# Transposing attention outputs by DMA instead of TensorE, with a new order for the first two batches

## The chip, the cores and the metric

One core of a Trainium2 chip. The metric is the device time of one execution in microseconds (us). "Span" is the time from first to last instruction in a profiled execution; the time measured from outside is some 2 us longer. A TensorE clock that the throttle lowers is shown in the profile as "PEclk".

## The reference, cut to what matters

```python
# q, k, v: [8 batches, 8 heads, 576 positions, 64]; 16 beacon keys and values for each head
scores = q @ concat(beacon_k, k).T / 8          # causal for k, the beacons are always visible
x = softmax(scores) @ concat(beacon_v, v)       # -> [4608 tokens, 512]
h = x @ w_in                                    # 512 -> 2048
out = maximum(0.01 * h, h) @ w_out              # 2048 -> 512
```

## The kernel before: the parts that matter

The kernel handles two heads at a time; such a group is called g0 to g31, four to a batch. Attention gives `x_nat`, with tokens in the partitions. The first feed-forward product needs `xT`, with channels in the partitions, so each group is transposed once: five TensorE transposes into PSUM (the memory that TensorE writes its results to), one VectorE copy out.

```python
def x_transposes(g):
    b, hp = divmod(g, NPAIR)
    x_nat, _ = xs.pop(g)
    ps = ps_one.tile([128, 1024], BF16, name="tp", tag="one")
    for t, (q0, rows) in enumerate(QT):      # QT: (0,112) (112,128) (240,128) (368,128) (448,128)
        nc.tensor.transpose(ps[:, q0:q0+rows], x_nat[0:rows, t]..., ident[0:rows, 0:rows])
    nc.vector.tensor_copy(out=xT[:, hp, b*S:(b+1)*S], in_=ps[:, 0:S])
```

The feed-forward part is cut into "fills", each four matmuls of 512 columns, which the schedule places between attention steps so that TensorE always has work. A fill of the first product reads `xT` of all four groups of a batch, so it may only be placed after that batch is released (`ready`).

```python
def fill():
    ...
    can1 = i1 < ready[0] and (i1 < 2 or i2 > i1 - 2)    # first product of chunk i1 (512 tokens)
    can2 = i2 < NCH and i2 < i1                         # second product of an earlier chunk
    ...
def finish(g):
    x_transposes(g)
    if hp == NPAIR - 1:
        ready[0] = NCH if b == B - 1 else b + 1
# for g: score(g); finish(g-3); value(g-2); t_q(g+1); masks(g), and fills in eight slots from g6 on
```

The kernel fixes the order of each engine's instructions by hand. SyncE's queue carries the loads of v and the stores of results (36 of 128x512 float32). GpSimd's queue carries the loads of q, k and the weights.

The softmax here doesn't subtract the row's maximum and nothing guards it: scores larger than these inputs give would overflow.

## Time and profile before

| | before |
|---|---|
| median time of 4 executions | 378.03 us (377.18 to 380.02) |
| span of the profiled execution | 375.6 us, mean granted clock 0.995 |
| TensorE wait for `xT` (copied by VectorE) | 2.1 us in all |
| filled group, eight fills | 9.81 us |
| unfilled group | 3.86 us |

A filled group is a group of attention with eight fills in it, an unfilled one has none. The prediction below shows the lines behind most of this table and reads them.

### The profile page before, as it was taken

To read this page: it belongs to the slowest core of one execution; us is meant where nothing else is said; L and a number is where in the kernel's file an instruction comes from. 1 tells how busy PE (TensorE), PEld (TensorE's weight loads), DVE (VectorE), ACT (ScalarE), POOL (GpSimd) and SP (SyncE) were. 2 spreads that over 40 slices of the span, in tenths; PEclk is the share of its full clock that TensorE was granted. 3 is DMA by queue.
4 is the path that set the end of the run, shared out by engine and by line. 5 is a ranking of instruction groups with operands and counts; after the bars stand their busy time and mean duration, and the time that the engine had idled before them with its cause. 6 is when DMAs were issued, how large, how long until landed. Compare 5 with 4: busy or idle time off the path is not lost.

```text
span 375.6 us, 7715 instructions
## 1 busy us (share of the span) xinstructions
PE 356.3 (95%) x3264; PEld 187.5 (50%) x3264; DVE 172.8 (46%) x402; ACT 195.4 (52%) x308; POOL 103.5 (28%) x143
## 2 busy tenths in 40 slices
PE   4887899999998899999999999999999999999996
PEld 4565464444555455555554555555554554444442
DVE  2779742243558645555456536644554332000021
ACT  3948574376436684368634763487336701643300
POOL 8569226684204802171208202300000000000000
PEclk9999899999999999999999999999999999999999
DMA  8997999959119910178015901100010011001012
GB/s 173 171 223 119 197 203 191 210 107 152 60 61 226 168 18 30 54 125 163 3 58 115 198 2 57 58 2 2 28 58 30 1 45 70 0 0 58 28 56 84
DMA packets 58370, 33.82 MB, mean 90 GB/s; under 512 B 41440, under 2 KB 53472, under 8 KB 58336
## 3 DMA queue, kind: packets, MB, share of 16 engines
q0 software_dynamic: 13152, 13.34, 22.8%
q1 hardware_dynamic: 44896, 19.67, 21.3%
q8 instruction: 25, 0.41, 0.5%
q10 hardware_dynamic: 288, 0.33, 0.3%
q14 instruction: 9, 0.07, 0.1%
HBM read 37.22 MB, written 9.44 MB: 124 GB/s over the span
## 4 chain that ended last, share of the span: by engine, by line
PE 86%; DVE 7%; DMA 3%; POOL 2%; SPq 1%; issue 1%; ACT 0%
PE acc L385 34%; PE acc L369 33%; PE av L333 7%; PE sc L267 6%; PE tp L244 4%; PE tp L355 2%; DMA v_raw<-in_k_dram 1%; DMA v_raw<-in_v_dram 1%; DVE osb L394 1%; DVE xT L360 1%; POOL q_raw L137 1%; DVE x_nat L343 1%; DVE qT L249 1%; SPq L216 1%; DVE kT L249 1%; DVE aT L299 1%
## 5 line engine op out<-in xcount | busy, mean ns | idle before, releaser
L369 PE MATMUL acc<-xT,w_in_sb 128*128 128x512 bf16 x576 | 140.6, 380 | 2.1 <-DVE xT L360 2.1
L278 ACT ACTIVATE aT<-sc 128x928 bf16<-128x928 f32 (+2 forms) x128 | 102.3, 855 | 75.9 <-PE sc L267 75.8
L385 PE MATMUL acc<-w_out_sb,gT 128*128 128x512 bf16 x576 | 139.1, 379 | 0.0
L376 ACT ACTIVATE gT<-acc 128x512 bf16<-128x512 f32 x144 | 85.7, 600 | 81.9 <-PE acc L369 81.8
L369 PEld LDWEIGHTS <-w_in_sb 128*128 128x128 bf16 x576 | 52.4, 98 | 59.8 <-issue 3.8
L385 PEld LDWEIGHTS <-gT 128*128 128x128 bf16 x576 | 52.1, 98 | 60.0 <-issue 5.3
L394 DVE COPY osb<-acc 128x512 f32<-128x512 f32 x36 | 24.8, 690 | 93.5 <-PE acc L385 93.1
L267 PE MATMUL sc<-qT,kT 64*128 64x128 bf16 (+5 forms) x384 | 42.6, 309 | 6.9 <-DVE kT L249 3.3
L333 PEld LDWEIGHTS <-aT 128*128 128x128 bf16 (+1 forms) x960 | 38.9, 100 | 16.5 <-issue 3.2
L333 PE MATMUL av<-v_aug,aT 128*128 128x65 bf16 (+1 forms) x960 | 42.0, 197 | 1.1 <-DVE xT L360 0.8
L167 POOL COPY q_nat<-q_raw 128x1152 bf16<-128x1152 bf16 (+1 forms) x16 | 18.3, 1145 | 82.5 <-PE tp L244 52.2
L249 DVE COPY qT<-tp 128x576 bf16<-128x576 bf16 x32 | 24.2, 755 | 33.7 <-PE tp L244 33.7
L343 DVE TENSOR_TENSOR x_nat<-av,rec 128x384 bf16<-128x384 f32 x64 | 31.4, 491 | 2.2
L267 PEld LDWEIGHTS <-kT 64*128 64x128 bf16 (+1 forms) x384 | 18.1, 100 | 21.1 <-issue 11.9
L225 POOL CAST v_aug<-v_raw 128x512 bf16<-128x512 f32 (+1 forms) x30 | 19.4, 683 | 33.5 <-PE av L333 31.5
L360 DVE COPY xT<-tp 128x576 bf16<-128x576 bf16 x32 | 14.5, 452 | 29.4 <-PE tp L355 29.4
L342 DVE RECIPROCAL rec<-av 128x6 f32<-128x6 f32 x64 | 11.8, 185 | 33.1 <-PE av L333 33.1
L137 POOL DMA_DIRECT2D q_raw<-in_q_dram x31 | 20.7, 669 | 12.3 <-DMA v_raw<-in_v_dram 4.5
L249 DVE COPY kT<-tp 128x576 bf16<-128x576 bf16 x31 | 23.2, 748 | 0.0
L299 DVE TENSOR_TENSOR aT<-aT,mask 128x768 bf16<-128x768 bf16 x32 | 22.6, 705 | 1.3 <-ACT aT L278 1.3
L137 POOL DMA_DIRECT2D k_raw<-in_k_dram x31 | 19.6, 632 | 7.4 <-DMA w_out_sb<-in_moe_w_out_dram 5.6
L167 POOL COPY k_nat<-k_raw 128x1152 bf16<-128x1152 bf16 (+1 forms) x16 | 18.5, 1157 | 0.9 <-DMA k_raw<-in_k_dram 0.9
(33 smaller groups left out, 149.7 us busy)
## 6 DMA issues: line engine op xcount, KB each, us to landing
out_dram<-osb SPq DMA_DIRECT2D x36, 256.0 KB, 2.0
v_raw<-in_v_dram SPq DMA_DIRECT2D x24, 256.0 KB, 6.2
q_raw<-in_q_dram POOLq DMA_DIRECT2D x31, 144.0 KB, 6.0
k_raw<-in_k_dram POOLq DMA_DIRECT2D x31, 144.0 KB, 6.2
w_in_sb<-in_moe_w_in_dram POOLq DMA_DIRECT2D x4, 512.0 KB, 8.6
w_out_sb<-in_moe_w_out_dram POOLq DMA_DIRECT2D x4, 512.0 KB, 16.8
v_raw<-in_v_dram SPq DMA_DIRECT2D x8, 224.0 KB, 4.6
v_raw<-in_v_dram SPq DMA_DIRECT2D x8, 160.0 KB, 5.1
```

The costliest lines, as they stand in the source:

```text
L137: dma = nc.gpsimd.dma_start(out=dst[e * RP : (e + 1) * RP], in_=src[b, h0 : h0 + 2].rearrange("h (p i) d -> p h i d", i=RI),)
L167: copy(out=dst[p0:p1], in_=src[p0:p1].rearrange("p h i d -> p i h d"))
L249: copy(out=dst.rearrange("c (p i) -> c p i", i=RI), in_=ps[:, 0:S].rearrange("c (i p) -> c p i", i=RI),)
L267: nc.tensor.matmul(out=sc[0 : ROWS[c], par, col - c0 : col - c0 + w], lhsT=kT[ps_, c * 128 : c * 128 + ROWS[c]], rhs=qT[ps_, q0 : q0 + w], ...
L278: last = nc.scalar.activation(out=aT[:, :, c0 : c0 + w], in_=sc[:, :, 0:w], func=AF.Exp, scale=0.125)
L299: nc.vector.tensor_tensor(out=diag, in0=diag, in1=tri[:, None, None, :].to_broadcast([128, 2, 3, 128]), op=ALU.mult,)
L333: nc.tensor.matmul(out=avv[:, n, 0 : D + 1], lhsT=aT[0 : ROWS[c], par, a0 : a0 + 128], rhs=va[0 : ROWS[c], c, 2 * hp + par, :], start=(c = ...
L343: nc.vector.tensor_tensor(out=x_nat[:, t0:t1].rearrange("p t e d -> p (t e) d"), in0=avv[:, :, 0:D], in1=rec[:, n0:n1, None].to_broadcast( ...
L369: nc.tensor.matmul(out=acc, lhsT=w_in_sb[:, j, fc * 128 : (fc + 1) * 128], rhs=xT[:, j, i * 512 : (i + 1) * 512], start=(j == 0), stop=(j ...
L376: nc.scalar.activation(out=gT[i][:, fc, :], in_=acc, func=AF.Prelu, alpha=0.01)
L385: nc.tensor.matmul(out=acc, lhsT=gT[i][:, fc, t * 128 : (t + 1) * 128], rhs=w_out_sb[:, fc, :], start=(fc == 0), stop=(fc == NF - 1),)
L394: nc.vector.tensor_copy(out=osb, in_=acc)
```

## The change

The intent is to take 160 transposes off TensorE and 32 copies off VectorE by letting DMAs that transpose while they copy (called the crossbar here) write `xT` straight from `x_nat`. To leave the DMAs time, a batch is released one group later, and the first eight groups and the v load of batch 2 are put in a new order.

```diff
-        ps = ps_one.tile(...)
-        for t, (q0, rows) in enumerate(QT):
-            nc.tensor.transpose(...)
-        nc.vector.tensor_copy(out=xT[:, hp, b * S : (b + 1) * S], in_=ps[:, 0:S])
+        flat = x_nat.rearrange("p t e d -> p t (e d)")
+        dst = xT[:, hp, b * S : (b + 1) * S]
+        nc.sync.dma_start_transpose(out=dst[:, None, 0:112], in_=flat[0:112, 0])
+        nc.sync.dma_start_transpose(
+            out=dst[:, 112:496].rearrange("p (t q) -> p t q", t=3),
+            in_=flat[:, 1:4].rearrange("p t x -> p (t x)"),
+        )
+        nc.sync.dma_start_transpose(out=dst[:, None, 448:576], in_=flat[:, 4])
...
-                ready[0] = NCH if b == B - 1 else b + 1
+                nxt[0] = NCH if b == B - 1 else b + 1     # ready[0] = nxt[0] at the next group
...
+            if g < 2 * NPAIR:        # new order of the first eight groups
+                score(g, 0); score(g, 1); t_q(g+1); value(g-2, 0); score(g, 2); score(g, 3)
+                value(g-2, 1); finish(g-3); masks(g)     # fills only from g7 on, in effect
```

(The last lines are condensed. Also: a third `x_nat` buffer; half of the first kT copies on ScalarE; `load_v(2)` after `finish(7)` instead of in g3; the casts of v for batches 1 and 2 and the transposes of the beacon keys also move by a group or so.)

More of the change, by code (lines that the diff above doesn't have):

```diff
@@ L319, in value @@
             xs[g] = (
-                headpool.tile([128, 5, 2, D], BF16, name="x_nat"),
+                headpool.tile([128, 5, 2, D], BF16, name="x_nat", bufs=3),
                 headpool.tile([128, 10], FP32, name="rec"),
@@ L352, in x_transposes @@
         x_nat, _ = xs.pop(g)
-        ps = ps_one.tile([128, 1024], BF16, name="tp", tag="one")
-        for t, (q0, rows) in enumerate(QT):
-            nc.tensor.transpose(
-                ps[:, q0 : q0 + rows],
-                x_nat[0:rows, t].rearrange("p e d -> p (e d)"),
-                ident[0:rows, 0:rows],
-            )
-        nc.vector.tensor_copy(out=xT[:, hp, b * S : (b + 1) * S], in_=ps[:, 0:S])
+        flat = x_nat.rearrange("p t e d -> p t (e d)")
[6 more added lines that the diff above has]
+        nc.sync.dma_start_transpose(out=dst[:, None, 448:576], in_=flat[:, 4])
     gT = {}
@@ L471, in loads @@
                 for i in range(4):
-                    w = load_w_out(i)
-                load_v(2, after=w)
+                    load_w_out(i)
                 load_qk(2, 0)
@@ L484, in loads @@
                         permute(b + 1, hp - 2, which, nc.gpsimd.tensor_copy)
-                if hp == 3:
+                if hp == 3 and b > 1:
                     cast_v(b + 1, nc.gpsimd)
@@ L492, in finish @@
             if hp == NPAIR - 1:
-                ready[0] = NCH if b == B - 1 else b + 1
-        for g in range(NG + 3):
+                nxt[0] = NCH if b == B - 1 else b + 1
+        nxt = [0]
+        for g in range(NG + 4):
+            ready[0] = nxt[0]
             if has(g):
@@ L517 @@
                 finish(g - 1)
+                load_v(2)
+                ready[0] = nxt[0]
                 for n in range(16):
@@ L535 @@
                 masks(g)
+                cast_v(2, nc.gpsimd)
                 fill()
+                continue
+            if g < 2 * NPAIR:
+                score(g, 0)
+                score(g, 1)
+                if g == 3:
+                    beacon_transposes(1, B)
+                if g + 1 < 2 * NPAIR:
+                    t_q(g + 1, 0)
+                    t_q(g + 1, 1, nc.scalar.copy if g % 2 else nc.vector.tensor_copy)
+                slot(2)
+                if g != 2 and has(g - 2):
+                    value(g - 2, 0)
+                slot(3)
+                score(g, 2)
+                score(g, 3)
+                if g == 2:
+                    cast_v(0, nc.vector)
+                    value(0, 0)
+                slot(5)
+                if has(g - 2):
+                    value(g - 2, 1)
+                slot(6)
+                if g == NPAIR:
+                    cast_v(1, nc.vector)
+                if has(g - 3):
+                    finish(g - 3)
+                masks(g)
                 continue
@@ L543 @@
             slot(0)
-            if g == 2:
-                cast_v(0, nc.vector)
-            if g == NPAIR + 1:
-                cast_v(1, nc.vector)
             if has(g - 3) and not 2 * NPAIR < g <= 2 * NPAIR + 2:
@@ L564 @@
             slot(5)
-            if g == 2:
-                beacon_transposes(1, B)
             slot(6)
```

## The prediction

> **What bounds the kernel now.** I read the page's busy shares and its chain of waits first.
>
> ```profile
> PE 356.3 (95%) x3264; PEld 187.5 (50%) x3264; DVE 172.8 (46%) x402; ACT 195.4 (52%) x308; POOL 103.5 (28%) x143
> ...
> PE 86%; DVE 7%; DMA 3%; POOL 2%; SPq 1%; issue 1%; ACT 0%
> PE acc L385 34%; PE acc L369 33%; PE av L333 7%; PE sc L267 6%; PE tp L244 4%; PE tp L355 2%; DMA v_raw<-in_k_dram 1%; DMA v_raw<-in_v_dram 1%; DVE osb L394 1%; DVE xT L360 1%; POOL q_raw L137 1%; DVE x_nat L343 1%; DVE qT L249 1%; SPq L216
> ```
>
> TensorE carries 86% of the chain, two thirds of the span with the feed-forward product alone. The transposes that the change removes (tp L355) are 2% of it. "Busy" counts each matmul's latency, so I took real cost from starts in the timeline of TensorE (start, us, what), in a group of heads in the steady part:
>
> ```profile
> 131.61 1.04 PE L369 MATMUL acc<-xT,w_in_sb 128*128 128x512 bf16 x4
> 132.48 0.44 PE L355 MATMUL tp<-ident,x_nat 112*128 112x112 bf16 x5
> 132.76 1.03 PE L369 MATMUL acc<-xT,w_in_sb 128*128 128x512 bf16 x4
> ```
>
> Five transposes hold the queue for 132.76 - 132.48 = 0.28 us. A "fill" (four 512-column matmuls) holds it 0.865 us (330.33 to 331.19, and so on in the tail). Then the windows view, one row for each group g of two heads, cut at its first score matmul (window, length, busy us of TensorE, weight loads, VectorE, ScalarE, GpSimd, granted clock, DMA share, GB/s):
>
> ```profile
> 23.69:29.84 6.15, 5.01 (x68) 3.78 (x67) 5.94 (x12) 3.47 (x5) 3.67 (x4) 1.00 0.91 164
> 29.84:33.70 3.86, 3.14 (x67) 2.22 (x67) 3.79 (x12) 3.38 (x5) 3.86 (x6) 1.00 0.52 73
> 33.70:39.23 5.53, 3.19 (x65) 2.35 (x67) 5.46 (x17) 3.39 (x5) 5.26 (x6) 0.95 1.24 205
> 39.23:46.88 7.65, 7.65 (x81) 4.19 (x82) 5.37 (x16) 5.26 (x8) 1.18 (x2) 0.81 1.23 195
> 46.88:52.62 5.74, 5.74 (x65) 3.09 (x65) 2.61 (x8) 5.42 (x9) 1.23 (x3) 1.00 1.23 203
> ...
> 117.11:120.97 3.86, 3.15 (x65) 2.37 (x67) 3.79 (x12) 3.49 (x6) 0.94 (x3) 1.00 1.25 253
> 120.97:131.09 10.12, 9.11 (x93) 4.74 (x94) 7.20 (x16) 6.94 (x11) 8.69 (x15) 1.00 1.07 172
> 131.09:140.90 9.81, 9.81 (x99) 5.13 (x99) 4.16 (x11) 7.81 (x13) 0.97 (x1) 1.00 0.15 25
> ```
>
> There are two regimes. A group with eight fills lasts 9.81 us and TensorE never idles. A group without fills (29.84, 117.11) lasts 3.86 us, VectorE busy for 3.79 of it: VectorE is the limit there, ScalarE next at 3.4 to 3.5, while TensorE's own attention work is about 9.81 - 8 x 0.865 = 2.9 us. So the removed matmuls count in the filled groups, the removed VectorE copies in the others.
>
> **What the Trainium skill says.** "VectorE: DVE Perf Modes", The three transpose paths, gives 390 ns for a TensorE transpose of 128x128 and 1309 ns for the DMA crossbar. The trace has 218 ns median latency per transpose and only 0.28 / 5 = 0.056 us of queue time, so the saving is far smaller than the page's duration suggests. For the crossbar this trace has nothing. "DMA: Bandwidth & Descriptors", Latency and other measured facts, gives 261 GB/s for one transposing kernel: 147 KB for a group is then an estimated 0.6 us plus a fixed part, against 9.8 us between groups. The same page, Issuing engines are not separate DMA queues, says all queues interleave on the same 16 engines. The trace agrees: 256 KB to the output lands in 2.0 us median when the engines are idle, a 256 KB piece of v takes 6.2 us. "TensorE: Matmul & The Clock Gate", Part 1, says the array runs at half rate until it has been busy some 3.4 us. The trace fits: nine q transposes start over 0.48 us at 25.91 (to 26.38) and 0.27 us at 31.10 (to 31.37), though the granted clock reads 1.00 in both windows.
>
> **The change part by part.** *Removed:* 160 transposes, 32 x 0.28 = 9.0 us of TensorE queue, nearly all in the path; and 32 VectorE copies of 0.452 us, 14.5 us in all, hidden except in unfilled groups, where one takes 0.37 us of the sequence (31.09 to 31.46). *Added:* 96 transposing DMAs on SyncE's queue, three per group. The third overlaps the second's destination (448 to 495) and by the build's order waits for it, so a group's SyncE chain is about one landing plus issue; I guess 3 to 4 us under load. *Moved:* batch 2's v load goes behind the last of batch 1's transposes; half of the first groups' kT copies go to ScalarE (0.64 us); scores go ahead of values; and a batch's transposed outputs are released one group later.
>
> That delay moves fills. Walking the counters of the schedule: before, no fills in g0 to g5, four each in g6 and g7, four in g12, none in g13, seven in g14. After: none in g0 to g6, four in g7, eight in g12, none in g13 and g14. Both have given 64 fills when g13 starts; after has still given 64 when g15 starts, which is where before stands at g14.
>
> I build the end time from the windows:
> 1. To g4. It cannot start much before 29.84: batch 1's first k block is only permuted by GpSimd at 24.78 + 1.15 = 25.93, behind its load, and that load is not moved. I take 29.3.
> 2. g4 to g6, no fills, VectorE the limit: 3 x (3.86 - 0.37) + 1.68 (v cast) - 0.67 (one kT copy to ScalarE) = 11.5; with 0.5 for a cold array g7 starts at 41.3. Before it was 46.88 with four more fills done, worth 3.5.
> 3. g7: 5.74 - 0.28 = 5.46, so g8 at 46.8 (before 52.62).
> 4. g8 to g12: before 117.11 - 52.62 = 64.5; less five transposings (1.4), less an idle 0.74 of the half-starved g12, plus the four late fills (3.46): 65.8. g13 at 112.6.
> 5. g13, g14 unfilled: 2 x 3.5 = 7.0. g15 at 119.6.
> 6. The rest: before, 375.6 - 120.97 = 254.6 from g14 with the same fills to go. Less one group's attention, 9.81 - 6.92 - 0.28 = 2.6; less 21 transposings, 5.9; less 1.2 of TensorE waits for the VectorE copy of xT (1.01 in g14 and 0.22 at 317): 244.9. End at 364.5.
>
> I add 1.5 for waits on transposing DMAs at g7 and in g8: 366.0 of span. Time exceeded span by 377.99 - 375.6 = 2.4, so 368.4, rounded to 368: 2.6% faster.
>
> **The rivals.** *(a) The transposes land late in the head.* The DMA share reads 0.9 to 1.2 there, and the first fill in g7 (about 42) needs groups 0 to 3. Their chain starts behind batch 1's v (issued until 22.9); my guess lands group 3 at about 43. If a chain takes 6 to 7 us instead, group 3 lands near 52 and group 7 near 77 (needed near 60 plus the first delay): 10 to 15 us lost, time 378 to 385. For it: congestion, and a chain of dependent DMAs. Against it: the crossbar moves half the bytes of one 256 KB load, and three x_nat buffers decouple it. *(b) Longer starvation lets the array go cold*, as at 39.23, where four fills and a group took 7.65 us at clock 0.81. Seven unfilled groups at the start and two in a row later could cost 2 to 4 us: 370 to 372. *(c) The gain is hidden:* if VectorE or DMA arrivals set the filled stretch, nothing is saved. The 9.81 us row with TensorE at 9.81 and VectorE at 4.16 speaks against it. *(d) The head gains more:* scores ahead of values and the later beacon transposes could remove the hole at 21.3 to 22.8; 364. Step 1's load speaks against it.
>
> **Range and chances.** The 9 us are well founded; the head is worth about +2 minus DMA waits. Rivals (b) and (d) give 364 to 372, (a) a tail above. Range 362 to 377; 2% faster means below 370.4. Chances: faster 0.64, same 0.27, slower 0.09.
>
> **What would show it.** In the page after: no L355 matmuls and no xT copy; a filled group at 9.5 us; g7, g13 and g15 near 41, 113 and 120; unfilled groups near 3.5. A TensorE wait for the transposes of xT over 3 us in g7 or g8 makes (a) right; two groups near 4.5 at g13 and g14, or matmuls at half rate there, make (b) right. A filled group still at 9.8 would make the prediction wrong at its root.

## The result

The changed kernel takes 407.38 us (406.5 to 409.89, four executions) against 378.03 us. The ratio is 1.0779 (95% interval 1.0713 to 1.0844): 7.8% slower. A ratio is always the mean time of one kernel's fast runs over that of the other's in the same rounds, so it is not quite the ratio of the medians quoted here.

First the page of the changed kernel: busy shares, the time line of TensorE and its clock in 40 slices of 10.2 us, the chain that ended last, and the costliest matmul group.

```profile
PE 351.7 (86%) x3059; PEld 180.4 (44%) x3104; DVE 158.5 (39%) x367; ACT 197.0 (48%) x311; POOL 101.5 (25%) x143
...
PE   5776305949999991999999999999999999999996
...
PEclk9999555997999995799999999999999999999999
...
PE 71%; DMA 13%; DVE 6%; SPq 5%; ACT 2%; issue 2%; DVEq 0%; ACTq 0%
...
L369 PE MATMUL acc<-xT,w_in_sb 128*128 128x512 bf16 x555 | 142.2, 390 | 35.5 <-DMA xT<-x_nat 33.9
```

The last of these lines in the kernel before:

```profile
L369 PE MATMUL acc<-xT,w_in_sb 128*128 128x512 bf16 x576 | 140.6, 380 | 2.1 <-DVE xT L360 2.1
```

TensorE's share of the chain fell from 86% to 71%, and DMA with SyncE's queue now hold 18%. The last line of the changed page says where: the first product's matmuls stood idle 35.5 us, 33.9 of them waiting for transposing DMAs. Before, they waited 2.1 us for VectorE's copy. In slices 5 to 7 and 16 the granted clock is 0.5 and TensorE is at most half busy.

The timeline of TensorE (start, us, what, idle before) shows the first fill in g7. Its four matmuls read groups 0, 1, 2 and 3 in turn:

```profile
43.31 0.61 PE L369 MATMUL acc<-xT,w_in_sb 128*128 128x512 bf16 x1
49.09 0.58 PE L369 MATMUL acc<-xT,w_in_sb 128*128 128x512 bf16 x1 [5.18 <-DMA xT<-x_nat]
59.06 0.58 PE L369 MATMUL acc<-xT,w_in_sb 128*128 128x512 bf16 x1 [9.39 <-DMA xT<-x_nat]
66.03 0.59 PE L369 MATMUL acc<-xT,w_in_sb 128*128 128x512 bf16 x1 [6.39 <-DMA xT<-x_nat]
```

Each waits for one group's transposes: 5.18 + 9.39 + 6.39 = 21.0 us in one fill. The queue of SyncE in the same time shows why. L355, L356 and L360 are a group's three transposing DMAs; a row's length is the time of issue:

```profile
33.16 1.27 SPq L355 DMA_TRANSPOSE xT<-x_nat  x1
34.52 1.27 SPq L356 DMA_TRANSPOSE xT<-x_nat  x1
43.65 1.11 SPq L360 DMA_TRANSPOSE xT<-x_nat  x1
44.84 1.18 SPq L355 DMA_TRANSPOSE xT<-x_nat  x1
46.12 1.21 SPq L356 DMA_TRANSPOSE xT<-x_nat  x1
53.63 1.11 SPq L360 DMA_TRANSPOSE xT<-x_nat  x1
54.79 1.23 SPq L355 DMA_TRANSPOSE xT<-x_nat  x1
```

The third transpose overwrites columns 448 to 495 of the second, so it is issued only after the second has landed, that is, after its data have arrived: 34.52 + 1.27 = 35.79 to 43.65 is 7.9 us, then 47.33 to 53.63 is 6.3 us. A group occupies the queue for about 10 us (44.84 to 54.79), while an unfilled group of attention here lasts 3.4 us (28.31 to 31.71). Late in the kernel the same landing takes 1.2 us (from 128.86 + 1.24 = 130.10 to 131.26):

```profile
128.86 1.24 SPq L356 DMA_TRANSPOSE xT<-x_nat  x1
131.26 1.12 SPq L360 DMA_TRANSPOSE xT<-x_nat  x1
```

The windows view (columns as in the prediction) tells what differs:

```profile
46.10:53.60 7.50, 0.58 (x1) 0.11 (x1) 1.92 (x6) 0.00 (x0) 1.77 (x3) 0.50 1.24 201
128.90:131.30 2.40, 2.35 (x23) 1.27 (x22) 0.75 (x2) 0.91 (x2) 0.00 (x0) 1.00 0.25 51
...
146.41:149.76 3.35, 2.88 (x62) 2.01 (x62) 2.85 (x6) 2.92 (x4) 0.08 (x1) 1.00 0.19 39
174.59:184.10 9.51, 9.40 (x91) 4.85 (x92) 4.12 (x10) 7.81 (x13) 2.24 (x2) 1.00 0.44 84
```

During the slow landing the DMA engines move 201 GB/s, nine tenths of it weights and batch 2's q and k (1.35 of 1.51 MB are from GpSimd's queue); during the quick one, 51. The last two rows answer to the prediction's regimes: an unfilled group went from 3.86 to 3.35 us and a filled one from 9.81 to 9.51. The intended saving is there; it is 0.3 us for a filled group.

Two later stretches cost as well. Around g8 TensorE waits 1.26 + 4.44 = 5.7 us, for groups 6 and 7. In g15, which follows two groups without fills, it waits 7.24 us for group 11:

```profile
86.93 0.39 PE L369 MATMUL acc<-xT,w_in_sb 128*128 128x512 bf16 x1 [1.26 <-DMA xT<-x_nat]
91.76 0.61 PE L369 MATMUL acc<-xT,w_in_sb 128*128 128x512 bf16 x1 [4.44 <-DMA xT<-x_nat]
...
163.85 0.61 PE L369 MATMUL acc<-xT,w_in_sb 128*128 128x512 bf16 x1 [7.24 <-DMA xT<-x_nat]
```

The transposes hold back VectorE too. A buffer of `x_nat` comes free only when its group's last transpose has landed, and VectorE waited for the buffers of groups 0 and 1:

```profile
38.96 0.56 DVE L343 TENSOR_TENSOR x_nat<-av,rec 128x384 bf16<-128x384 f32 x1 [2.12 <-DMA xT<-x_nat]
49.07 0.56 DVE L343 TENSOR_TENSOR x_nat<-av,rec 128x384 bf16<-128x384 f32 x1 [6.65 <-DMA xT<-x_nat]
```

### The profile page after: what moved, and what is told of

It is laid out like the page before. It is cut to its first block, busy times and chain, and to the rows that moved or that the text cites. A ratio compares the mean times of both kernels' runs of the same rounds, so it can differ in the third digit from the quotient of the medians.

```text
span 408.2 us, 7536 instructions
## 1 busy us (share of the span) xinstructions
PE 351.7 (86%) x3059; PEld 180.4 (44%) x3104; DVE 158.5 (39%) x367; ACT 197.0 (48%) x311; POOL 101.5 (25%) x143
## 3 DMA queue, kind: packets, MB, share of 16 engines
q1 hardware_dynamic: 67936, 24.79, 26.7%
## 4 chain that ended last, share of the span: by engine, by line
PE 71%; DMA 13%; DVE 6%; SPq 5%; ACT 2%; issue 2%; DVEq 0%; ACTq 0%
PE acc L385 29%; PE acc L369 28%; DMA xT<-x_nat 12%; PE av L333 5%; PE sc L267 5%; PE tp L244 4%; SPq L355 2%; SPq L360 2%; ACT aT L278 2%; DMA v_raw<-in_k_dram 1%; DVE v_aug L225 1%; DVE x_nat L343 1%; SPq L216 1%; DVE aT L299 1%; DVE qT L249 1%
## 5 line engine op out<-in xcount | busy, mean ns | idle before, releaser
L369 PE MATMUL acc<-xT,w_in_sb 128*128 128x512 bf16 x555 | 142.2, 390 | 35.5 <-DMA xT<-x_nat 33.9
L385 PE MATMUL acc<-w_out_sb,gT 128*128 128x512 bf16 x552 | 134.5, 382 | 1.6 <-issue 0.5
L369 PEld LDWEIGHTS <-w_in_sb 128*128 128x128 bf16 x576 | 53.9, 100 | 101.5 <-issue 31.4
L385 PEld LDWEIGHTS <-gT 128*128 128x128 bf16 x576 | 53.0, 98 | 64.2 <-issue 6.8
L137 POOL DMA_DIRECT2D q_raw<-in_q_dram x31 | 19.4, 627 | 13.7 <-DMA v_raw<-in_v_dram 4.5
L249 DVE COPY kT<-tp 128x576 bf16<-128x576 bf16 x28 | 21.0, 749 | 0.0
L244 PEld LDWEIGHTS <-q_nat 64*128 64x128 bf16 x288 | 11.6, 100 | 11.3 <-issue 9.7
## 6 DMA issues: line engine op xcount, KB each, us to landing
w_in_sb<-in_moe_w_in_dram POOLq DMA_DIRECT2D x4, 512.0 KB, 10.2
```

The lines of the kernel that those rows point to most:

```text
L137: dma = nc.gpsimd.dma_start(out=dst[e * RP : (e + 1) * RP], in_=src[b, h0 : h0 + 2].rearrange("h (p i) d -> p h i d", i=RI),)
L244: nc.tensor.transpose(ps[:, i * RP : (i + 1) * RP], nat[b, grp][which][ps_, i].rearrange("p h d -> p (h d)"), ident[ps_, ps_],)
L249: copy(out=dst.rearrange("c (p i) -> c p i", i=RI), in_=ps[:, 0:S].rearrange("c (i p) -> c p i", i=RI),)
L369: nc.tensor.matmul(out=acc, lhsT=w_in_sb[:, j, fc * 128 : (fc + 1) * 128], rhs=xT[:, j, i * 512 : (i + 1) * 512], start=(j == 0), stop=(j ...
L385: nc.tensor.matmul(out=acc, lhsT=gT[i][:, fc, t * 128 : (t + 1) * 128], rhs=w_out_sb[:, fc, :], start=(fc == 0), stop=(fc == NF - 1),)
```

## The experiments

| run | what it is | time, us | ratio to before (interval) |
|---|---|---|---|
| changed | the change as given | 407.38 | 1.0779 (1.0713 to 1.0844) |
| e1 | crossbar alone, old order | 481.42 | 1.2724 (1.2660 to 1.2789) |
| e2 | new order alone | 376.16 | 0.9936 (0.9893 to 0.9980) |
| e3 | changed, four transposes without overlap | 402.10 | 1.0623 (1.0568 to 1.0677) |
| e4 | new order, crossbar from batch 3 on, late release | 378.79 | 1.0002 (0.9952 to 1.0051) |
| e5 | crossbar for batches 0 and 1 only | 405.84 | 1.0725 (1.0682 to 1.0768) |
| e6 | changed, six weight loads replaced by memset | 401.97 | 1.0610 (1.0557 to 1.0664) |
| e7 | crossbar where a filled group lies before the use | 372.07 | 0.9827 (0.9798 to 0.9857) |
| e8 | e7 with the overlapping three | 372.00 | 0.9834 (0.9797 to 0.9871) |
| e9 | changed, loads kept away from groups 2 and 3 | 402.75 | 1.0613 (1.0564 to 1.0663) |
| e10 | changed, batch 3's v load later | 401.09 | 1.0573 (1.0516 to 1.0631) |
| e11 | e10 and e3 together | 391.51 | 1.0343 (1.0285 to 1.0401) |
| e12 | e7 with batch 2 as well | 376.49 | 0.9939 (0.9904 to 0.9974) |

My theory after the result: the transposes reach TensorE late, because SyncE's queue is a chain of issue and landing, and because the landing shares the DMA engines with loads. The rivals: the new order is to blame, or the crossbar is slow whenever transposes follow each other.

### e1 and e2: each half alone

e1 is the kernel before with the three transposing DMAs and the third `x_nat` buffer, and nothing else. e2 is the changed kernel with this edit:

```diff
-        (three dma_start_transpose)
+        (the five TensorE transposes and the VectorE copy of before)
...
                 nxt[0] = NCH if b == B - 1 else b + 1
+                ready[0] = nxt[0]
```

> The crossbar transposes alone, in the order of the kernel before (batch 2's v load still issued from SyncE in group 3, ahead of the transposes and behind the last w_out load). Theory A (the transposes stand in SyncE's queue, and TensorE's first fills wait for that queue): no transpose can be issued before w_out has landed (about 56 us in the trace of before) and batch 2's v is issued (some 8 us more), so the first fill waits until roughly 85 to 95 us in place of 41; time 410 to 430. Rival B (the loss comes from the changed order, not from the queue): below 390.

> The changed order alone: every transpose is back on TensorE and VectorE, with a batch released as soon as its transposes are issued, all else as in the changed kernel. Theory A (the order is harmless): 374 to 379, within 1.5% of before; the prediction's own sum gave it about 2 us of gain without the crossbar. Rival B (seven groups without fills and a cold array cost the 29 us): above 390.

e2 took 376.16 us: the order is harmless, even 0.6% faster, and its group 7 starts at 42.54 us in place of 46.88. So the loss comes with the crossbar. (e2 also takes the later release back. No run has the later release with TensorE's transposes; but the 33.9 us that TensorE waits for transposing DMAs are more than the 31 us between e2 and the changed kernel.)

e1 took 481.42 us, the right direction but far beyond 410 to 430. The first part went as expected. Batch 2's v load, waiting for w_out, stood at the head of SyncE's queue until 57.01 us, and the first transpose was issued at 64.85. VectorE sat 34.39 us waiting for a free `x_nat` buffer, and the first fill was complete at 89.75. What I missed is that the old order releases each batch at once, so that later batches wait again: TensorE's first-product matmuls waited 61.9 us for transposes in the whole run. The changed kernel, with the later release and the moved v load, is 74 us faster than e1; how much each of the two is worth was not separated.

### e3: no overlap between the transposes

```diff
-            out=dst[:, 112:496].rearrange("p (t q) -> p t q", t=3),
-            in_=flat[:, 1:4].rearrange("p t x -> p (t x)"),
+            out=dst[:, 112:368].rearrange("p (t q) -> p t q", t=2),
+            in_=flat[:, 1:3].rearrange("p t x -> p (t x)"),
         )
+        nc.sync.dma_start_transpose(out=dst[:, None, 368:448], in_=flat[0:80, 3])
         nc.sync.dma_start_transpose(out=dst[:, None, 448:576], in_=flat[:, 4])
```

> The changed kernel with four transposing DMAs for a group in place of three, none of which overlaps another's destination, so that SyncE issues them without waiting for a landing. Theory A1 (the chain of issue, landing and next issue, about 10 us for a group in the head, is what makes the data late): a group then takes about 4 x 1.15 = 4.6 us of the queue, group 3 lands near 50 in place of 66, TensorE's waits for xT fall from 34 to below 18 us, time 385 to 394. Theory A2 (the transposes share the DMA engines with the weight loads and get too little of them, whatever the chain): landings grow as more of them are in flight, waits stay above 28 us, time 402 to 410.

The waits, 25.6 us, lie between the two theories; the time, 402.10 us, lies in the range of A2, so A1's forecast of 385 to 394 us missed. The first fill was complete at 54.63 us in place of 66.03, so the chain was worth 11 us there. In the queue a group now takes 5.1 us (44.95 to 50.06) with no wait at all: four issues of about 1.2 us. That is still longer than the 3.4 us of an unfilled group, and the last three groups of the first fill became complete 4.6 to 4.9 us apart (45.11, 49.73, 54.63), so here the issue itself has become the limit. Then the gain was lost again. The load of batch 3's v, which stands in the queue between the transposes of groups 4 and 5, held it for 13.6 us (from 55.13), and group 8 waited 3.33 + 1.17 + 4.64 us.

### e4: crossbar from batch 3 on

The edit is e2's with TensorE's transposes only `if b < 3`, e3's four DMAs otherwise, and immediate release only for `b < 3`.

> Crossbar transposes without overlap only from batch 3 on, TensorE's for batches 0 to 2 (with immediate release), the order of the changed kernel. Theory A (they hide wherever loads do not crowd and a group lasts 9.5 us): 20 groups x 0.28 = 5.6 us are saved against the order alone, a filled group takes 9.5 us, time 368 to 373. Rival C (they disturb outputs and loads on SyncE's queue in the steady part too): 376 or more.

A miss: 378.79 us. Filled groups did take 9.5 us (201.55 to 211.09). But the change from immediate to late release, at batch 3, leaves one group without fills, and the next then needs group 15 sooner than the queue delivers it:

```profile
163.51 0.59 PE L267 MATMUL sc<-qT,kT 64*128 64x512 bf16 x4 [0.88 <-ACT aT L282]
164.03 0.82 PE L383 MATMUL acc<-xT,w_in_sb 128*128 128x512 bf16 x3
172.22 2.31 PE L383 MATMUL acc<-xT,w_in_sb 128*128 128x512 bf16 x5 [7.37 <-DMA xT<-x_nat]
```

This is about the same wait as in g15 of the changed kernel, and the start-up loads are long over. The unfilled group before it lasts 4.4 us (159.07 to 163.51) in place of 9.5, which shortens the time that the DMA has to hide in. But the DMA share in the wait was 1.17 (163.5 to 172.2, beside loads of q and k), so a slow landing may have its part; e4 does not separate the two, and e12 below is the cleaner case.

### e5: crossbar for batches 0 and 1 only

Edit: TensorE's transposes and immediate release `if b >= 2`.

> Crossbar transposes, as in the changed kernel, for batches 0 and 1 only; TensorE's transposes and immediate release from batch 2 on. Theory A (the loss is made in the head, where nothing but the weight and q/k loads is in the way): TensorE's waits for transposing DMAs stay near the 27 us that the changed kernel shows in groups 7 and 8, the array goes to half rate there as well, and the time is 376 + 27 + 2 to 6 = 400 to 410. Rival B (the later batches, or outputs queued behind transposes, cost as much): below 392.

405.84 us, as theory A said; TensorE waited 20.3 us in g7 (3.93 + 9.37 + 6.97) and 5.4 us in g8. So the 29 us that separate the changed kernel from before are made by the transposes of the first eight groups. From batch 2 on, the crossbar's gain, an estimated 24 x 0.28 = 6.7 us, and the 7.24 us wait nearly cancel.

### e6: fewer loads, by memset

```diff
-                    load_w_in(i)                     # i = 1, 2, 3
+                    nc.gpsimd.memset(w_in_sb[:, :, i * 512 : (i + 1) * 512], 0.0)
```

and the same for three of the four w_out loads. The result is wrong.

> The changed kernel with six of the eight weight loads replaced by a GpSimd memset of the same tile (wrong result on purpose): some 6.3 MB less to read while the first transposes are in flight, queue and chain unchanged. Theory A2 (the transposes are slow because they share the 16 DMA engines with these loads): the second transposes of groups 1 to 3 land in 1.5 to 3 us after their issue in place of 6 to 8, the waits at group 7 fall from 21 us to below 10, time below 396. Theory A3 (a transpose straight after another on the queue is slow in itself): landings stay at 6 to 8 us, time 402 to 408.

The time says nothing, because the edit brought a stall of its own. VectorE's cast of v met the memsets on GpSimd:

```profile
32.32 13.03 DVE L225 CAST v_aug<-v_raw 128x512 bf16<-128x512 f32 x5
```

Before, the same five casts took 1.76 us. TensorE stood idle 12.55 us before g6 for this, and g7 started only at 51.65. The Trainium skill, "SBUF — State Buffer", SBUF: two separate sides, describes an exclusive lock on a port pair that GpSimd shares with VectorE's two-port modes, held for a whole instruction; 13.03 us beside memsets that ran from 32.27 to 43.56 fits that, though no run shows in which mode the cast ran. The landings did shorten: 2.5 us for group 1 and 2.9 us for group 2, in place of 7.9 and 6.3. Group 3, beside q and k loads, still took 5.3. So e9 repeats the question without memsets.

### e7 and e8: crossbar only where a filled group lies between

```diff
+    def by_pe(b, hp):
+        return b < 3 or hp == NPAIR - 1
     def x_transposes(g):
+        if by_pe(b, hp):
+            (TensorE transposes and VectorE copy)
+            return
...
+                if by_pe(b, hp):            # always true for a batch's last pair
+                    ready[0] = nxt[0]
```

e7 uses e3's four transposes, e8 the changed kernel's three.

> Crossbar transposes (four to a group, none overlapping) only for the first three pairs of heads of batches 3 to 7; TensorE's for batches 0 to 2 and for each batch's last pair, so that a batch is released at once. Theory A (they hide where a group of 9.5 us lies between them and their use): no TensorE wait for a transposing DMA above 1 us, 15 x 0.28 = 4.2 us less than the order alone, 371 to 374 us. Rival C (outputs and v loads on the same queue delay them past their use): waits for xT of 2 us or more, 376 or more.

> The same as the kernel with four transposing DMAs, but with the changed kernel's three, the third waiting for the second's landing. Theory A: the wait costs nothing where loads do not crowd, so the time is within 1 us of that kernel's. Rival: the chain (3.5 us of issue and a landing of up to 8 us beside the q and k loads) reaches past the use, and it is 2 us or more slower.

Both hit: 372.07 and 372.00 us, faster than before by 1.7%, the best. In e7 no TensorE wait for a transposing DMA remains among those that the trace lists. (The intervals, 0.9798 to 0.9857 and 0.9797 to 0.9871, lie wholly below 1; whether the gain reaches 2% they leave open.) Against e2 the ratio falls from 0.9936 to 0.9827, about 1.1% or 4.1 us, as 15 x 0.28 = 4.2 us says. With a filled group to hide in, the wait inside the chain costs nothing: e8 equals e7. The changed kernel shows the same: a second transpose issued by 197.29 landed only at 203.96, 6.7 us later at a DMA share of 1.24, and no wait of TensorE follows.

### e9: the loads kept away

The first quarter of each weight is loaded and stands for all four (`fc % 4`), and batch 2's q and k wait for group 3's last transpose. Wrong result, no memset.

> The changed kernel with the loads taken out of the way of groups 0 to 3 without any memset: only the first quarter of each weight is loaded and stands for all four (wrong result on purpose), and batch 2's q and k are loaded only after group 3's last transpose has landed. Theory A2 (sharing the DMA engines is what stretches the landings): the second transposes of groups 1 to 3 wait about 1.2 to 2.9 us for their landing in place of 6.3 to 7.8, a group takes 4.8 to 6 us of the queue, TensorE's waits in group 7 fall from 21 to 4 to 8 us, time 386 to 396. Theory A3 (chained transposes are slow in themselves): landings above 5 us, waits in group 7 above 14 us, time above 400.

```profile
43.41 1.18 SPq L355 DMA_TRANSPOSE xT<-x_nat  x1
44.68 1.22 SPq L356 DMA_TRANSPOSE xT<-x_nat  x1
47.09 1.11 SPq L360 DMA_TRANSPOSE xT<-x_nat  x1
48.25 1.22 SPq L355 DMA_TRANSPOSE xT<-x_nat  x1
49.57 1.21 SPq L356 DMA_TRANSPOSE xT<-x_nat  x1
51.89 1.11 SPq L360 DMA_TRANSPOSE xT<-x_nat  x1
```

The window of these transposes, in the columns of the prediction:

```profile
43.00:50.00 7.00, 1.49 (x5) 0.30 (x3) 1.92 (x6) 1.69 (x2) 0.00 (x0) 0.71 0.16 33
```

This settles what stretches the landings. With the DMA share at 0.16 (window from 43 to 50), the second transposes of groups 2 and 3 landed 1.19 us (45.90 to 47.09) and 1.11 us after their issue, in place of 6.3, in the same chain and order. Group 1, beside the two weight loads that were left, still took 5.7 us. So the slow landing is the sharing of the DMA engines, not the chaining of transposes. A group still took 4.8 us of the queue, most of it issue, and group 7's waits fell from 21.0 to 9.8 us (1.03 + 4.41 + 4.35), a little above the 4 to 8 expected.

The time, 402.75 us, missed: the loads that I had moved came back in g7 and g8. Group 4 was slow beside q and k, batch 3's v load held the queue for 8.0 us (60.46 to 68.41), and g8 waited 0.64 + 4.41 + 4.23 = 9.3 us.

### e10 and e11: the v load that stood in the way

The changed kernel moves batch 2's v load behind group 7, but the loop issues batch 3's at the start of g8, ahead of the transposes of groups 5 to 7.

```diff
-                    if hp == 0:
+                    if hp == 0 and b > 2:
                         load_v(b + 1)
...
                 load_v(2)
+                load_v(3)
```

> The changed kernel with batch 3's v load moved in SyncE's queue from between the transposes of groups 4 and 5 to behind those of group 7 and batch 2's v. If the 4.7 us that this load holds the queue (73.28 to 77.97) lie in the path of group 8's waits, those fall from 5.7 us to about 1 and the time is 402 to 404; if the chain catches up otherwise, it stays at 406 to 408.

> Both repairs of the queue: four transposes without overlap, and batch 3's v load behind group 7's transposes. In the run with the first repair alone that load held the queue from 55.1 to 68.8 us, just ahead of group 5. If the queue is the limit, group 8's waits (9 us there) go to 3 us or less and the time is 391 to 396; if the shared DMA engines are, the loads lost time comes back elsewhere and it is above 398.

e10: 401.09 us, 6 to 8 us better than the changed kernel (6.3 by the medians, 7.8 by the ratios) and a little beyond the expectation; group 8's wait fell to 0.46 us. e11: 391.51 us, as the queue theory said, with no wait in g8 and 16.6 us of waits left, half of them in g7 and half in g15. By the ratios the two repairs bring 5.9 and 7.8 us alone and 16.5 together. That is not clearly more than their sum, 13.7, with intervals of some 2 us either way; that the second obstacle takes back what the first repair gains is seen in e3's trace (first fill 11 us earlier, time 5.9 us better), not in these times.

### e12: e7 with batch 2 as well

Edit: `return b < 2 or hp == NPAIR - 1`.

> The four-transpose hybrid with batch 2 too on the crossbar for its first three pairs. These are used at group 14, right after two groups with few or no fills. Theory (a transposing DMA hides only if a filled group of 9.5 us lies between it and its use): TensorE waits 2 to 6 us in group 14, and the time is 372 to 377, no better than without batch 2. Rival (the queue alone matters and is free there): no wait, 371.

```profile
124.72 0.59 PE L383 MATMUL acc<-xT,w_in_sb 128*128 128x512 bf16 x2 [3.16 <-DMA xT<-x_nat]
```

TensorE waited 3.16 us for group 10 in g14, and the time was 376.49 us. The loads are not at fault here: the DMA share was 0.41 (119.9 to 125.2), and the transpose that TensorE waited for was issued at 122.22 to 123.45 and had landed by 124.72. It was issued late: stores, a v load and group 9's transposes held the queue until 119.14, and the group before its use, without fills, lasted only 3.3 us (116.54 to 119.88). Three more groups on the crossbar cost 4.4 us against e7 instead of saving 3 x 0.28 us; 3.16 us of this is the wait, the rest was not traced.

## Why the prediction was wrong

**Its framework held.** TensorE's queue as the bound, 0.28 us for a group's transposes, two regimes: a filled group came out at 9.51 us (predicted 9.5), an unfilled one at 3.35 and, with a v cast on GpSimd and a 1.55 us wait, 4.87 (predicted 3.5). g7 started at 42.38 (41.3). The order was worth 0.6%, close to the 2 us of the sum.

**What failed is the term "I add 1.5 for waits on transposing DMAs at g7 and in g8".** It was mis-sized: the waits there were 21.0 + 5.7 = 26.7 us. Under it lies the guess that a group's SyncE chain is "one landing plus issue; I guess 3 to 4 us under load". The form was right, the sizes were not: it measured about 10 us, 3.5 us of issue alone (three times about 1.17) and landings of 6.3 to 7.9 us. I had no measured figure for the issue at all. Even with the engines nearly free, in e9, a group took 4.8 us, more than the guess for a loaded queue, and g7 still waited 9.8 us. The only figure that I had for the transfer was the 261 GB/s of the Trainium skill ("DMA: Bandwidth & Descriptors", Latency and other measured facts), an estimated 0.6 us for a group's 147 KB plus a fixed part. It says nothing of load: the 98 KB of a second transpose landed 1.1 to 1.2 us after their issue in e9 and 6.3 us beside the loads. I had seen the DMA share of 0.9 to 1.2 in these very windows, and did not apply it to the term.

**Rival (a) was the right one**, with its mechanism: transposes late in the head, for congestion (e9) and for the chain (e3). I gave it 378 to 385 us, taking a chain of 6 to 7 us with group 3 at 52 and group 7 at 77 us (measured: about 10 us, 66.0 and 91.8), and all of "slower" a chance of 0.09. Neither argument against it held: the bytes did not decide, as the same bytes landed 1.1 us after issue in e9 and 6.3 us here, and three `x_nat` buffers did not decouple the chain, as VectorE's waits of 2.12 and 6.65 us show. It also lacked the v load of batch 3 in the queue, worth 6 to 8 us (e10). I read only that batch 2's had been moved.

**Step 6 had no term for g15.** Group 11 is used after two groups with no fills, and TensorE waited 7.24 us; e4 and e12 show waits after unfilled groups too. The rest of the step came out: 244.9 us were predicted from g15 to the end and 253.6 measured (154.63 to 408.2), 246.3 without this wait.

**Rival (b)** was right in part: while TensorE waits, the granted clock is 0.50, and the next fills run at half rate (eight matmuls from 166.63 take 2.93 us, 1.89 later). But it comes with the waits and not with the unfilled groups: in e2, which has the same seven unfilled groups at the start and no transposing DMA, the granted clock reads 1.00 in each of g4 to g7 (30.10 to 48.43). In the changed kernel it reads 0.70 already in g6, after TensorE gaps of 1.86 and 1.57 us, the second behind VectorE's wait for a buffer; the two unfilled groups at g13 did not go cold (1.00). The sum from g7 to g8 shows it: predicted 5.46, measured 29.6 (42.38 to 72.00), of which 21.0 are waits and some 3 us the slow clock and its like.

**Still open:** how the 7.24 us at g15 divide between the queue (stores and v loads stand ahead of groups 8 to 10) and the shared engines (group 11's second transpose took 5.5 us to land, at a DMA share of 1.00). No run separated the two. e11, with both repairs, still stands 15 us above e2, with 16.6 us of waits; no form of the crossbar for the first batches came out even.

## What to carry to other kernels

A DMA that replaces compute work has a latency and a queue: before trusting it, multiply its issue time, and where one transfer waits for another also its landing time *under the load of that stage*, by the number of transfers in a row, and compare with the rhythm of the consumer. Here it paid only where a full stage of other work lay between its producer and its consumer, with the old path kept for the start-up and for each batch's last piece (e7). Read the issuing engine's whole order, not only the diff: loads and stores that stand ahead in the same queue delay it as well.

## What the Trainium skill lacked or had wrong

- "DMA: Bandwidth & Descriptors" has no issue time for SBUF-to-SBUF transposing DMAs of this size on this chip, only cycle counts of one large case of "previous generations". Here an issue on SyncE took 1.1 to 1.3 us in most cases (medians 1.18, 1.21 and 1.11 for 112, 384 and 128 rows, single ones up to 3.2), so three or four for a group are 3.5 to 5.1 us of queue.
- The same page's 261 GB/s for transposing DMAs has no warning about load: the landing of 98 KB after issue was 1.1 to 1.2 us with the engines nearly free (e9) and 4.0 to 7.9 us beside traffic of 137 to 201 GB/s (groups 1 to 4 of the changed kernel).
- "VectorE: DVE Perf Modes" compares 390 ns (TensorE) with 1309 ns (crossbar) for 128x128. As durations they mislead for a full pipeline: five TensorE transposes held the queue for 0.28 us in all.
